# A fused attention and expert kernel on one Trainium2 core: v's two local heads on blocks of 32 partitions, zero halves kept in place, the strided weights reordered by the multiplication with 1/sum

## The chip, the cores and the metric

The kernel runs on one core of one Trainium2 chip. The metric is the device time in microseconds (us), the median of several runs. Beside the runs, one execution was taken by the hardware profiler; its times, and the views worked out from it, are what this document calls the profile. Engines: PE multiplies matrices (PEld is its weight load), DVE, ACT and POOL work element by element, SP issues the DMAs (SPq is its queue).

## What is computed

Attention with 8 batches of 8 heads (576 positions, 64 wide), the first four heads with a window of 32 positions ("local"), the other four with every 32nd position ("strided"). Then a layer of 8 experts (w1, w2) with a capacity of 80 rows each; a row goes to its best expert or stays zero.

```python
def _attn_ref(q, k, v):                      # B, H, S, D = 8, 8, 576, 64
    scores = scale * np.matmul(q, k.transpose(0, 1, 3, 2))
    mask_local = (rel >= 0) & (rel < 32)
    mask_strided = (rel >= 0) & (pos[None, :] % 32 == pos[:, None] % 32)
    masks = np.stack([mask_local if h < H // 2 else mask_strided for h in range(H)], axis=0)
    scores = np.where(masks[None, :, :, :], scores, -1000000000.0)
    scores = scores - np.max(scores, axis=-1, keepdims=True)
    attn = np.exp(scores)
    attn = attn / (np.sum(attn, axis=-1, keepdims=True) + 1e-09)
    return np.matmul(attn, v).astype(np.float32)

def _moe_ref(x, w_gate, w1, w2, capacity):   # x: 4608 x 512, 8 experts, 1024 wide, capacity 80
    logits = x @ w_gate
    expert_idx = np.argmax(logits, axis=1)
    ...
    for e in range(E):
        ...                                  # the 80 rows of e with the largest gate weight
        h = np.maximum(x[tok_idx] @ w1[e], 0.0)
        out[tok_idx] = gate_w[tok_idx, None] * (h @ w2[e])
```

## The kernel before

**Stages.** For each of the 8 batches: q and k are loaded (L617, L620) into `raw` buffers; for the local heads pairs of heads are interleaved by a copy (L401 on POOL, L403 on DVE); PE transposes them (L646), and the transposes are moved from PSUM by ACT or DVE. k is stored twice, each time with the other head's 64 partitions zero, by a multiplication with the 0/1 columns `km` (`masked`: one ACT instruction for each half, L410, or one DVE instruction for both, L417). Local scores (L726 and L735) and strided scores (L809, L816) go through the same `softmax`: the row maximum is subtracted, ACT takes the exp (L692), DVE the row sum (L693) over the weights and a column that holds 1e-9, then 1/sum (L695), and DVE or POOL multiplies (L703). The weights are transposed (L760 local, L834 strided), moved from PSUM with `masked` once more (by `um` local, by `hm` strided), and multiplied with v (L783, L855). The logits of the experts follow (L870, L876), and the output rows are transposed (L952) and stored to a DRAM tensor `xs` (L975, L997).

**v.** For the local heads v lies in one buffer, `vlb`. Its partitions 64 to 127 hold 32 positions each of two heads, and its partitions 0 to 63 the same one block of 32 positions earlier, so that one product covers the window. Eight DMAs of 80 or 64 KB in packets of 256 bytes load it (L671), and a copy fills the lower half from the upper (one for each of two parts, L401 or L403). The two heads alternate from partition to partition: head `u` is written to partitions `64 + u`, `66 + u` and so on. For the strided heads, v goes to 72 partitions next to each other (L683).

**Experts.** The 64 chunks of w1 and w2 (L578, L580) are split into two float16 halves, high (L590 on ACT, L592 on POOL) and low (L598 and L599 on POOL, L601 on DVE). 20 chunks are split before the choice of the rows (from about 417 us), the others between the matrix products of the experts (L1212 to L1214).

**What sets the order.** `program` lists all operations with their readers, writers, a rank and the time that each engine is thought to need (`t_pool`, `t_dve`, `PAR`); `plan` goes through them, gives each the engine that can begin it first and a buffer, and so fixes the order on every engine in advance. `emit` then writes the instructions in that order. All buffers of `program` are pieces of one tile, `K.arena`; the semaphore waits between instructions are put in afterwards, by the framework, from the regions of the tile that each instruction reads and writes.

Of the kernel before, what the change touches and what calls it, by code (L numbers as in the profile page):

```python
# [9 lines left out]
BF16 = mybir.dt.bfloat16  # L10
# [249 lines left out]
def t_pool(n, x=0.0):  # L260
    return 0.15 + 0.001 * n + x
# [6 lines left out]
def program(K, par):  # L268
# [14 lines left out]
    def pool(name, n, count, fifo=True):  # L283
        return Pool(name, [flat(carve(n), n) for _ in range(count)], fifo)
# [17 lines left out]
    plp = pool("pl", 650, 3)  # L302
    psp = pool("ps", 304, 3)
    r4 = end[0]
# [8 lines left out]
    lts = pool("lt", 288, 4)  # L313
    gas = pool("ga", 360, 2)
# [57 lines left out]
    hm, um, km, sel16 = c("hm"), c("um"), c("km"), c("sel16")  # L372
# [33 lines left out]

    def masked(e, o, i, m, n):
# [43 lines left out]
    def c5(e):  # L451
        e.tensor_reduce(K.hm, K.ident.rearrange("p (s z) -> p z s", z=4), op=ALU.add, axis=AX.X)
        e.tensor_reduce(K.um, K.ident.rearrange("p (s z) -> p z s", z=2), op=ALU.add, axis=AX.X)
# [6 lines left out]
    dve(0.9, c5, [ident], [hm, um, km], -99)  # L460
# [6 lines left out]
    def ceps(e):  # L467
        for p in plp.aps:
            e.memset(p().rearrange("p (c n) -> p c n", n=130)[:, :, 128:130], EPS)
        for p in psp.aps:  # L470
            e.memset(p().rearrange("p (g n) -> p g n", n=76)[:, :, 72:76], EPS)

    pol(0.9, ceps, [], [eps], -58)
    pol(0.2, lambda e: e.memset(K.arena[:, kto:kto + 32], 0.0), [], [c("pad")], -90)
    pol(0.4, lambda e: e.memset(vlb().rearrange("p (t h d) -> p t h d", h=2, d=D)[0:64, 0], 0.0), [],  # L475
        [(vlb, "z")], -57)
# [55 lines left out]
    tk = static(lambda: K.tk)  # L532
# [102 lines left out]
    def transposes(src, g, which, rank):  # L635
# [4 lines left out]
        for j3 in range(3):  # L640
# [7 lines left out]
            pe(0.335, f, [src, ident], [t], rank + 0.01 * j3, 128, claim=[dst])  # L648

            def ev(e, t=t, j3=j3):  # L650
# [11 lines left out]
            else:  # L662
                add([("ACT", 1.05), ("DVE", 0.95)], ev, [t, km], [(dst, j3)], rank + 0.5 + 0.01 * j3)
        return dst

    def loadv(b, rank_l, rank_s):
        v4 = lambda: vlb().rearrange("p (t h d) -> p t h d", h=2, d=D)
        for m, (t0, t1) in enumerate(VT):
            for u in range(2):
                for h in range(2):  # L670
                    dma(2.75 * (t1 - t0) / 72, lambda e, u=u, h=h, t0=t0, t1=t1: e.dma_start(  # L671
                        v4()[64 + u:128:2, t0:t1, h],
# [16 lines left out]
    def softmax(p, mx, parts, n, view, ps, rank, tt):  # L689
# [3 lines left out]
        dve(t_dve(tt * 1.02), lambda e: e.tensor_reduce(sm()[:, 0:n], view("eps"), op=ALU.add, axis=AX.X),  # L693
            [p, eps], [sm], rank + 1)
        dve(0.18, lambda e: e.reciprocal(sm()[:, 0:n], sm()[:, 0:n]), [sm], [sm], rank + 1.2)  # L695

        def mul(e):
# [3 lines left out]
            if len(pv.shape) == 4:  # L701
                s = s.rearrange("p (c u) -> p c u", u=pv.shape[2])
            eng.tensor_tensor(pv, pv, s.unsqueeze(len(s.shape)).broadcast_to(list(pv.shape)), op=ALU.mult)  # L703

        add([("POOL", t_poolb(tt) if tt != 288 else 0.66), ("DVE", t_dve(tt))], mul, [p, sm], [p], rank + 1.5)

    def local_scores(b, it, qt, kt, rank):
# [4 lines left out]
        def view(kind):  # L712
            a = p()[:, 0:130 * (t1 - t0)].rearrange("p (c n) -> p c n", n=130)
            if kind == "all":
                return a[:, :, 0:128]
            a = a.rearrange("p c (k u) -> p c u k", u=2)
            return a[:, :, :, 0:64] if kind == "p" else a

        for j, (c0, c1) in enumerate(CGR[it]):
            s = bank()  # L720

            def f(e, s=s, c0=c0, c1=c1):
                w = 128 * (c1 - c0)
# [18 lines left out]
            sv = lambda s=s, w=w: s()[:, 0:w].rearrange("p (t c) -> p t c", c=64)  # L742
# [3 lines left out]
                view("p")[:, c0 - t0:c1 - t0], s()[:, 0:w].rearrange("p (c u k) -> p c u k", u=2, k=64),  # L746
                mx()[:, o:o + nn].rearrange("p (c u) -> p c u", u=2).unsqueeze(3).broadcast_to([P, c1 - c0, 2, 64]),
# [4 lines left out]
    def local_values(b, it, p, xl, rank):  # L752
        t0, t1 = CGR[it][0][0], CGR[it][-1][1]
        pt = Buf(pls_)
        for j, (c0, c1) in enumerate(CGR[it]):
            t = bank()

            def f(e, t=t, c0=c0, c1=c1):
                for cc in range(c0, c1):
                    e.transpose(t()[:, P * (cc - c0):P * (cc - c0) + P],  # L760
                                p()[:, 130 * (cc - t0):130 * (cc - t0) + 128], K.ident)
# [9 lines left out]
            add([("ACT", 2 * t_act(n) - 0.1), ("DVE", t_dve(2 * n))], ev, [t, um], [(pt, j)], rank + 0.5 + 0.2 * j)  # L771
        for j, (c0, c1) in enumerate(CGR[it]):
# [14 lines left out]
            vr = [(vlb, ("p", m)) for m in ms] + [(vlb, ("o", m, u, h)) for m in ms for u in range(2) for h in range(2)]  # L787
# [697 lines left out]
```

## Time and profile before

| | us |
|---|---|
| median of 3 runs | 537.05 |
| lowest, highest | 536.18, 541.28 |
| the profiled execution | 540.64 |
| its span (first to last instruction) | 538.9 |
| PE, DVE, ACT, POOL busy in it | 294.7, 255.4, 189.1, 210.0 |
| mean clock granted to PE | 0.731 |

The span has five stages: the first loads (to about 40 us), the batches (to 417), the choice of the rows for each expert (to 440), the experts (to about 530) and the last store. A busy time is the union of an engine's instructions; matrix products overlap, and their ends are modelled. Idle time before an instruction is put down to the event that came last, here written "<- engine, tile, line", "DMA arena<-v" for a load of v into the arena. In a table by stage, the columns are: from and to, length, busy time and number of instructions of each engine, granted clock, mean busy share of the 16 DMA engines, GB/s.

### The profile page before, as it was taken

To read this page: it belongs to the slowest core of one execution; us is meant where nothing else is said; L and a number is where in the kernel's file an instruction comes from. 1 tells how busy PE (TensorE), PEld (TensorE's weight loads), DVE (VectorE), ACT (ScalarE), POOL (GpSimd) and SP (SyncE) were. 2 spreads that over 40 slices of the span, in tenths; PEclk is the share of its full clock that TensorE was granted. 3 is DMA by queue.
4 is the path that set the end of the run, shared out by engine and by line. 5 is a ranking of instruction groups with operands and counts; after the bars stand their busy time and mean duration, and the time that the engine had idled before them with its cause. 6 is when DMAs were issued, how large, how long until landed. Compare 5 with 4: busy or idle time off the path is not lost. (4 is left out here: it accounts for less than half of the span.)

```text
span 538.9 us, 12588 instructions
## 1 busy us (share of the span) xinstructions
PE 294.7 (55%) x5344; PEld 264.9 (49%) x5344; DVE 255.4 (47%) x430; ACT 189.1 (35%) x334; POOL 210.0 (39%) x188
## 2 busy tenths in 40 slices
PE   3581295129405790285248318703975537997773
PEld 3570175028404680274247217703854437997773
DVE  1382165127313731274148315622695972996730
ACT  0341144033303331243136215311575403865521
POOL 3410083032023212142140222201077676999991
PEclk8596679558955865588659857855895656999886
DMA  6461086128204830194039207611978594887801
GB/s 200 122 245 24 15 271 202 23 74 275 97 22 133 252 128 22 31 314 140 22 92 330 65 13 237 221 24 29 311 240 278 183 327 142 247 291 275 273 26 41
DMA packets 56432, 84.26 MB, mean 156 GB/s; under 512 B 23346, under 2 KB 32564, under 8 KB 56372
## 3 DMA queue, kind: packets, MB, share of 16 engines
q1 hardware_dynamic: 55348, 80.79, 46.8%
q0 software_dynamic: 1024, 2.62, 1.6%
q8 instruction: 44, 0.72, 0.6%
q14 instruction: 16, 0.13, 0.1%
HBM read 63.21 MB, written 20.19 MB: 155 GB/s over the span
## 5 line engine op out<-in xcount | busy, mean ns | idle before, releaser
L401 POOL TENSOR_SCALAR arena<-arena 128x1152 f32<-128x1152 f32 (+3 forms) x30 | 31.5, 1053 | 110.4 <-DMA arena<-v 75.6
L952 PE MATMUL bank<-ident,arena 128*128 128x128 f32 x144 | 28.4, 345 | 78.7 <-DMA arena<-v 63.4
L599 POOL TENSOR_TENSOR arena<-arena 128x1024 f16<-128x1024 f32 x31 | 70.0, 2257 | 2.6
L1213 PE MATMUL bank<-arena 128*128 128x80 f16 x512 | 63.0, 211 | 4.9 <-DVE arena L1208 2.7
L1212 PE MATMUL bank<-arena 128*128 128x80 f16 x512 | 63.3, 211 | 3.6 <-issue 2.3
L1214 PE MATMUL bank<-arena 128*128 128x80 f16 x512 | 62.9, 211 | 2.8 <-POOL arena L599 2.8
L646 PE MATMUL bank<-ident,arena 128*128 128x128 f32 x288 | 56.0, 361 | 14.2 <-DVE arena L403 11.2
L601 DVE SCALAR_TENSOR_TENSOR arena<-arena 128x1024 f16<-128x1024 f32 x33 | 56.4, 1739 | 14.3 <-POOL arena L592 7.8
L952 PEld LDWEIGHTS bank<-ident,arena 128*128 128x128 f32 x144 | 22.1, 191 | 83.4 <-issue 82.9
L410 ACT ACTIVATE arena<-bank,km 128x384 f32<-128x384 f32 x68 | 38.8, 650 | 65.3 <-DMA arena<-v 39.6
L397 ACT COPY arena<-bank 128x512 f32<-128x512 f32 (+4 forms) x64 | 32.7, 513 | 79.5 <-DMA arena<-v 23.5
L1214 PEld LDWEIGHTS <-arena 128*128 128x128 f16 x512 | 54.1, 106 | 8.6 <-issue 5.2
L646 PEld LDWEIGHTS bank<-ident,arena 128*128 128x128 f32 x288 | 50.0, 195 | 15.7 <-POOL arena L475 11.4
L1212 PEld LDWEIGHTS <-arena 128*128 128x128 f16 x512 | 54.2, 106 | 2.6 <-issue 2.6
L1213 PEld LDWEIGHTS <-arena 128*128 128x128 f16 x512 | 54.2, 106 | 1.4 <-issue 1.3
L598 POOL TENSOR_SCALAR arena<-arena 128x1024 f32<-128x1024 f32 x31 | 38.5, 1241 | 39.6 <-DMA arena<-v 25.8
L834 PE MATMUL bank<-ident,arena 128*72 128x128 f32 x64 | 15.2, 385 | 64.5 <-DVE arena L703 64.4
L590 ACT ACTIVATE arena<-arena 128x1024 f16<-128x1024 f32 x44 | 44.6, 1054 | 16.6 <-DMA arena<-moe_w 12.7
L592 POOL TENSOR_SCALAR arena<-arena 128x1024 f16<-128x1024 f32 x20 | 26.4, 1320 | 52.1 <-DMA arena<-v 28.0
L693 DVE TENSOR_REDUCE arena<-arena 128x16 f32<-128x304 f32 (+2 forms) x32 | 23.1, 729 | 42.9 <-DMA arena<-v 42.8
L703 POOL TENSOR_TENSOR arena<-arena 128x288 f32<-128x288 f32 (+1 forms) x7 | 7.3, 1045 | 90.2 <-DMA arena<-v 55.2
L834 PEld LDWEIGHTS bank<-ident,arena 128*72 128x72 f32 x64 | 8.2, 154 | 67.9 <-ACT arena L399 36.6
(170 smaller groups left out, 597.8 us busy)
## 6 DMA issues: line engine op xcount, KB each, us to landing
arena<-moe_w SPq DMA_DIRECT2D x64, 512.0 KB
arena<-q SPq DMA_DIRECT2D x16, 576.0 KB
arena<-k SPq DMA_DIRECT2D x16, 576.0 KB
out<-arena SPq DMA_DIRECT2D x18, 512.0 KB
xs<-arena SPq DMA_DIRECT2D x16, 512.0 KB
arena<-v SPq DMA_DIRECT2D x16, 288.0 KB
arena<-v SPq DMA_DIRECT2D x32, 80.0 KB
arena<-v SPq DMA_DIRECT2D x32, 64.0 KB
```

Source lines behind the costliest of these rows:

```text
L397: K.nc.scalar.copy(o, i)
L401: K.nc.gpsimd.tensor_scalar(o, i, 1.0, 0.0, op0=ALU.mult, op1=ALU.add)
L410: K.nc.scalar.activation(o(z), i, AF.Copy, scale=m[:, z:z + 1])
L590: K.nc.scalar.activation(part(0), st(), AF.Copy, scale=SC)
L598: K.nc.gpsimd.tensor_scalar(st(), st(), SC, 0.0, op0=ALU.mult, op1=ALU.add)
L599: K.nc.gpsimd.tensor_tensor(part(1), st(), part(0), op=ALU.subtract)
L601: K.nc.vector.scalar_tensor_tensor(part(1), st(), SC, part(0), op0=ALU.mult, op1=ALU.subtract)
L646: e.transpose(t()[:, P * jj:P * jj + P], cp[:, 3 * j3 + jj], K.ident)
L952: e.transpose(t()[:, P * k:P * k + P], src[half][1](k), K.ident)
L1212: e.matmul(o, w[:, 0, i:i + P], x[:, 0], start=first, stop=False)
L1213: e.matmul(o, w[:, 0, i:i + P], x[:, 1], start=False, stop=False)
L1214: e.matmul(o, w[:, 1, i:i + P], x[:, 0], start=False, stop=last)
```

## The change

- **Local v.** Head `u` now lies on partitions `64 * u + 32` to `64 * u + 63`, and its earlier block on the 32 partitions below. The copy of the earlier block becomes two, one for each head. The columns of the local weights are ordered head by head (`(u k)`, not `(k u)`), so that their transposes fit; `um` goes, `km` serves.
- **Zero halves.** The halves of `ktl`, `kst` and `ptl` that are always zero are set once at the start. ACT then copies only the 64 partitions that differ (`halves_of`); DVE multiplies both halves as before.
- **1e-9.** The local weights lose their two extra columns a chunk (640 for 650 elements); 16 additions, one for each local softmax, add 1e-9 to the sums on DVE or POOL. Strided weights keep a column.
- **Strided weights.** They stay in the order of the scores until the multiplication with 1/sum, which writes them to a second buffer (`pq`) in the order that the transposes need.
- **Memory.** `oh` moves into the arena on top of `lt`, and `tk` onto `gates`.
- **Planner.** Its times for POOL and for two DVE multiplications change.

```diff
 def t_pool(n, x=0.0):
-    return 0.15 + 0.001 * n + x
+    return 0.1 + 0.00093 * n + x
...
-    plp = pool("pl", 650, 3)
+    plp = pool("pl", 640, 3)
     psp = pool("ps", 304, 3)
+    pqp = pool("pq", 288, 2)
...
+    def halves_of(e, o, i):
+        if e == "ACT":
+            for x in range(2):
+                K.nc.scalar.copy(o(x)[64 * x:64 * x + 64], i[64 * x:64 * x + 64])
+        else:
+            masked(e, o, i, K.km, 2)
...
+    for i, (o, n, rk) in enumerate(((kto + 32, 2 * S, -89), (kss.off, 2 * S, -56), (pls_.off, 640, -55),
+                                    (pls_.off + 1280, 640, -20))):
+        for x in range(2):
+            add([("POOL", t_pool(n)), ("DVE", 0.1 + 0.00055 * n)],
+                lambda e, o=o, n=n, x=x: (K.nc.gpsimd if e == "POOL" else K.nc.vector).memset(
+                    K.arena[64 * x:64 * x + 64, o + n * (1 - x):o + n * (2 - x)], 0.0), [], [(pads[i if i < 3 else 3], x)], rk)
...
-                    masked(e, lambda z: d if z is None else d[:, z], tv, K.km, 2)
+                    halves_of(e, lambda z: d if z is None else d[:, z], tv)
...
                     dma(2.75 * (t1 - t0) / 72, lambda e, u=u, h=h, t0=t0, t1=t1: e.dma_start(
-                        v4()[64 + u:128:2, t0:t1, h],
+                        v4()[64 * u + 32:64 * u + 64, t0:t1, h],
...
-            add([("POOL", t_pool(nn)), ("DVE", 0.1 + 0.00065 * nn)],
-                lambda e, a0=a0, t1=t1: copy(e, v4()[0:64, a0:t1], v4()[64:128, a0 - 1:t1 - 1]),
-                own, [(vlb, ("p", m))], rank_l + 3 + m * par["vm"])
+            for u in range(2):
+                add([("POOL", t_pool(nn)), ("DVE", 0.1 + 0.00065 * nn)],
+                    lambda e, a0=a0, t1=t1, u=u: copy(e, v4()[64 * u:64 * u + 32, a0:t1],
+                                                      v4()[64 * u + 32:64 * u + 64, a0 - 1:t1 - 1]),
+                    [x for x in own if x[1][2] == u], [(vlb, ("p", m, u))], rank_l + 3 + m * par["vm"])
...
-        dve(t_dve(tt * 1.02), lambda e: e.tensor_reduce(sm()[:, 0:n], view("eps"), op=ALU.add, axis=AX.X),
-            [p, eps], [sm], rank + 1)
+        if tt == 288:
+            dve(t_dve(tt * 1.02), lambda e: e.tensor_reduce(sm()[:, 0:n], view("eps"), op=ALU.add, axis=AX.X),
+                [p, eps], [sm], rank + 1)
+        else:
+            dve(t_dve(tt), lambda e: e.tensor_reduce(sm()[:, 0:n], view("sum"), op=ALU.add, axis=AX.X),
+                [p], [sm], rank + 1)
+            add([("DVE", 0.19), ("POOL", 0.22)], lambda e: (K.nc.gpsimd if e == "POOL" else K.nc.vector).tensor_scalar(
+                sm()[:, 0:n], sm()[:, 0:n], EPS, 0.0, op0=ALU.add, op1=ALU.add), [sm], [sm], rank + 1.1)
...
+            if ps is None:
+                eng.tensor_tensor(pv, pv, s.broadcast_to(list(pv.shape)), op=ALU.mult)
+            else:
+                o = ps().rearrange("p (g c z) -> p g z c", g=4, z=4)
+                i = pv.rearrange("p (g z) c -> p g z c", z=4)
+                s = s.rearrange("p (g z) o -> p g z o", z=4)
+                eng.tensor_tensor(o, i, s.broadcast_to([P, 4, 4, 18]), op=ALU.mult)
...
-            if kind == "all":
-                return a[:, :, 0:128]
-            a = a.rearrange("p c (k u) -> p c u k", u=2)
-            return a[:, :, :, 0:64] if kind == "p" else a
+            if kind == "all":
+                return a
+            return a.rearrange("p (t k) -> p t k", k=64)
...
-                masked(e, lambda z: d if z is None else d[:, z], tv, K.um, 2)
+                halves_of(e, lambda z: d if z is None else d[:, z], tv)
...
-    hiA=[("ACT", 1.06), ("POOL", 1.15)], loA=[("DVE", 1.39), ("POOL", 2.85)],
+    hiA=[("ACT", 1.06), ("POOL", 1.05)], loA=[("DVE", 1.39), ("POOL", 3.15)],
...
-    cp=[("POOL", 1.3), ("DVE", 0.85)],
+    cp=[("POOL", 1.25), ("DVE", 0.85)],
```

How this moves the instructions is seen in the order on each engine. In the rows below, "waits" names the semaphores that an instruction waits for: PE, DVE, Activation (ACT) and Pool for those engines, DMAHW0 to DMAHW7 for the eight lanes that SP's DMAs use in turn (the end _49 is part of the names). A number of lines is 29 or so higher in the changed kernel.

SP, the first loads, before (L617 and L620 load q and k, L671 v):

```order
L620 DMA arena<-q 128x1152
L620 DMA arena<-k 128x1152
L485 DMA wgt<-moe_w_gate 128x2x8 [waits DVE_49]
L671 DMA arena<-v 32x10x64 [waits DMAHW2_49,DMAHW3_49,DMAHW1_49,DMAHW0_49]
L671 DMA arena<-v 32x10x64 x3
L671 DMA arena<-v 32x8x64 x3
L671 DMA arena<-v 32x8x64 [waits DMAHW4_49,DVE_49,Pool_49]
```

The same place in the changed kernel (L634 and L637 load q and k, L689 v, L502 the gate's weights):

```order
L637 DMA arena<-q 128x1152
L637 DMA arena<-k 128x1152
L689 DMA arena<-v 32x10x64 x4
L689 DMA arena<-v 32x8x64 [waits DMAHW0_49]
L689 DMA arena<-v 32x8x64 [waits DMAHW1_49]
L689 DMA arena<-v 32x8x64 [waits DMAHW2_49]
L689 DMA arena<-v 32x8x64 [waits DMAHW3_49]
L502 DMA wgt<-moe_w_gate 128x2x8 [waits DMAHW4_49,DVE_49]
```

The first load of v stood behind the lanes of all four loads of q and k; now the first four loads of v have no wait, and the others wait for one lane each.

SP, the loads of v for the second batch, before, and the load of k behind them:

```order
L671 DMA arena<-v 32x10x64 [waits DMAHW1_49,DMAHW3_49,DMAHW0_49,DMAHW4_49,DVE_49,DMAHW5_49,PE_49,DMAHW7_49,Activation_49,Pool_49]
L671 DMA arena<-v 32x10x64 [waits DVE_49,Activation_49]
L671 DMA arena<-v 32x10x64 [waits Activation_49]
L671 DMA arena<-v 32x10x64 [waits DVE_49,DMAHW6_49,Activation_49,Pool_49]
L671 DMA arena<-v 32x8x64 [waits DVE_49,Activation_49]
L671 DMA arena<-v 32x8x64 [waits Pool_49]
L671 DMA arena<-v 32x8x64 [waits PE_49]
L671 DMA arena<-v 32x8x64 [waits DMAHW2_49,DVE_49,Activation_49]
L617 DMA arena<-k 128x2x576 [waits DMAHW4_49,DMAHW5_49,DMAHW3_49,DMAHW6_49,DMAHW2_49,DMAHW7_49,DMAHW1_49,DMAHW0_49]
```

and in the changed kernel (L569 writes zeros to the output):

```order
L689 DMA arena<-v 32x10x64 [waits DMAHW2_49,DVE_49,PE_49]
L689 DMA arena<-v 32x10x64 [waits DMAHW3_49,PE_49]
L689 DMA arena<-v 32x10x64 [waits DMAHW4_49]
L689 DMA arena<-v 32x10x64 [waits DMAHW5_49]
L689 DMA arena<-v 32x8x64 [waits DMAHW6_49,PE_49]
L689 DMA arena<-v 32x8x64 [waits DMAHW7_49,PE_49]
L689 DMA arena<-v 32x8x64 [waits DMAHW0_49]
L689 DMA arena<-v 32x8x64 [waits DMAHW1_49]
L569 DMA out<-arena 512x1x256 [waits DMAHW2_49]
L634 DMA arena<-k 128x2x576 [waits DMAHW3_49,Pool_49]
```

Each load waited for up to four engines; now four of the eight wait for PE, one of these for DVE too, and all for one lane.

DVE, the end of the first batch, from the strided scores on, before (L822 subtracts the maximum, L693 to L703 are the softmax, L417 masks):

```order
L822 TENSOR_TENSOR arena<-bank_82,arena 128x4x4x18 [waits DVE_49]
L822 TENSOR_TENSOR arena<-bank_75,arena 128x4x4x18 [waits DVE_49]
L403 COPY arena<-bank_80 128x2x128 [waits PE_49,Activation_49]
L693 TENSOR_REDUCE arena<-arena 128x16 [waits DMAHW7_49,DMAHW0_49,Activation_49]
L693 TENSOR_REDUCE arena<-arena 128x16 [waits DMAHW1_49,Activation_49,Pool_49]
L695 RECIPROCAL arena<-arena 128x16 [waits DVE_49] x2
L703 TENSOR_TENSOR arena<-arena 128x4x4x18 [waits DMAHW2_49,DVE_49]
L403 COPY arena<-arena 128x4x32 [waits DMAHW3_49,Activation_49]
L405 TENSOR_SCALAR arena<-bank_76 128x128x3 [waits DMAHW4_49,PE_49]
L417 TENSOR_TENSOR arena<-bank_77,hm 72x1152 [waits DMAHW5_49,PE_49]
L417 TENSOR_TENSOR arena<-bank_80,km 128x256x3 [waits DMAHW6_49,PE_49,Activation_49]
```

and in the changed kernel (L852, L714 to L734, L429):

```order
L852 TENSOR_TENSOR arena<-bank_79,arena 128x16x18 [waits DVE_49]
L408 COPY arena<-bank_78 128x2x128 [waits PE_49]
L851 TENSOR_REDUCE arena<-bank_77 128x16
L714 TENSOR_REDUCE arena<-arena 128x16 [waits Activation_49]
L852 TENSOR_TENSOR arena<-bank_77,arena 128x16x18 [waits DVE_49]
L721 RECIPROCAL arena<-arena 128x16 [waits DVE_49]
L734 TENSOR_TENSOR arena<-arena 128x4x4x18 [waits DVE_49]
L714 TENSOR_REDUCE arena<-arena 128x16 [waits Activation_49]
L721 RECIPROCAL arena<-arena 128x16 [waits DVE_49]
L734 TENSOR_TENSOR arena<-arena 128x4x4x18 [waits DVE_49]
L429 TENSOR_TENSOR arena<-bank_79,km 128x256x3 [waits PE_49]
L429 TENSOR_TENSOR arena<-bank_81,km 128x256x3 [waits PE_49]
```

The sums, multiplications and maskings named the lanes of DMAs one after the other (DMAHW7, 0, 1, 2 up to 6); now they name only the engines whose results they use. The copies of v's earlier block are 16 before, 10 of them on POOL and 6 on DVE, and 32 after, 15 on POOL and 17 on DVE. Of the 16 additions of 1e-9, 7 stand on POOL and 9 on DVE. Between the choice of the rows and the end POOL had 14 low and 7 high halves of the weights and has 13 and 6, DVE had 30 low halves and has 31.

More of the change, by code (lines that the diff above doesn't have):

```diff
@@ L283, in pool @@
     def pool(name, n, count, fifo=True):
-        return Pool(name, [flat(carve(n), n) for _ in range(count)], fifo)
+        off = end[0]
+        p = Pool(name, [flat(carve(n), n) for _ in range(count)], fifo)
+        p.off = off
+        return p
     def static(ap):
@@ L459, in program @@
     dve(0.15, lambda e: e.tensor_copy(K.identb, K.ident), [ident], [identb], -100)
-    dve(0.9, c5, [ident], [hm, um, km], -99)
+    dve(0.9, c5, [ident], [hm, km], -99)
     warm(par["warm0"], -200)
@@ L648, in transposes @@
             pe(0.335, f, [src, ident], [t], rank + 0.01 * j3, 128, claim=[dst])
+            zeros = [] if which == 0 else [pads[0], pads[0]] if g == 0 else [pads[1]]
             def ev(e, t=t, j3=j3):
@@ L662, in transposes @@
             else:
-                add([("ACT", 1.05), ("DVE", 0.95)], ev, [t, km], [(dst, j3)], rank + 0.5 + 0.01 * j3)
+                add([("ACT", 1.02), ("DVE", 0.96)], ev, [t, km, *zeros], [(dst, j3)], rank + 0.5 + 0.01 * j3)
         return dst
@@ L700, in mul @@
             s = sm()[:, 0:n]
[L701 to L705, printed above, removed]
+            s = s.unsqueeze(2)
+            if ps is None:
[5 more added lines that the diff above has]
+                eng.tensor_tensor(o, i, s.broadcast_to([P, 4, 4, 18]), op=ALU.mult)
+        if ps is None:
+            add([("POOL", t_poolb(tt)), ("DVE", 0.2 + 0.00105 * tt)], mul, [p, sm], [p], rank + 1.5)
+        else:
+            add([("POOL", 0.83), ("DVE", 0.68)], mul, [p, sm], [ps], rank + 1.5)
     def local_scores(b, it, qt, kt, rank):
@@ L760, in f @@
                     e.transpose(t()[:, P * (cc - c0):P * (cc - c0) + P],
[L761 removed]
+                                p()[:, P * (cc - t0):P * (cc - t0) + P], K.ident)
             pe(0.112 * (c1 - c0), f, [p, ident], [t], rank + 0.2 * j, 128, claim=[pt])
@@ L768, in ev @@
                 tv = t()[:, 0:P * (c1 - c0)].rearrange("p (c n) -> p c n", n=P)
-                masked(e, lambda z: d if z is None else d[:, z], tv, K.um, 2)
-            add([("ACT", 2 * t_act(n) - 0.1), ("DVE", t_dve(2 * n))], ev, [t, um], [(pt, j)], rank + 0.5 + 0.2 * j)
+                halves_of(e, lambda z: d if z is None else d[:, z], tv)
+            add([("ACT", 2 * t_act(n) - 0.1), ("DVE", t_dve(2 * n))], ev, [t, km, pads[2], pads[3]], [(pt, j)], rank + 0.5 + 0.2 * j)
         for j, (c0, c1) in enumerate(CGR[it]):
@@ L833, in f @@
             for g in range(4):
-                e.transpose(t()[0:72, P * g:P * g + P], p()[:, 76 * g:76 * g + 72], K.ident)
+                e.transpose(t()[0:72, P * g:P * g + P], p()[:, 72 * g:72 * g + 72], K.ident)
         pe(0.45, f, [p, ident], [t], rank, 128, claim=[pt])
@@ L1133, in program @@
         [(small, 0), (slot, "s"), jc], [(slot, "b")], z + 0.5)
-    oh, tab = c("oh"), bank()
+    oh, tab = Buf(Pool("oh", [None], True, [(lts,)])), bank()
     for j0 in (0, 8):
@@ L1305 @@
     vm=2.0, mstep=4.0, mx=2.0, mf=5.0, gland=6.3,
-    hiA=[("ACT", 1.06), ("POOL", 1.15)], loA=[("DVE", 1.39), ("POOL", 2.85)],
-    hiB=[("ACT", 1.06), ("POOL", 1.15)], loB=[("DVE", 1.39), ("POOL", 2.85)],
-    cp=[("POOL", 1.3), ("DVE", 0.85)],
+    hiA=[("ACT", 1.06), ("POOL", 1.05)], loA=[("DVE", 1.39), ("POOL", 3.15)],
+    hiB=[("ACT", 1.06), ("POOL", 1.05)], loB=[("DVE", 1.39), ("POOL", 3.15)],
+    cp=[("POOL", 1.25), ("DVE", 0.85)],
     rank=dict(lq=-16.0, cp=-6.0, tl=0.0, ls=-8.0, vl=-6.0, vs=0.0, sl=3.0, sx=1.0, ts=6.0, pl=8.0, pli=1.5, ss=10.0,
@@ L1341, in moe_attention @@
     mk(work, "identb", [P, P], BF16)
-    mk(work, "mloc", [P, 10, 64], BF16)
+    mk(work, "mloc", [P, 5, P], BF16)
     mk(work, "mstr", [P, 16, 18], BF16)
@@ L1345, in moe_attention @@
     K.wgl, K.wgs = K.wgt[:, 0], K.wgt[:, 1]
-    for name, n in (("hm", 4), ("um", 2), ("km", 2), ("sel16", 16), ("segm", NSEG), ("esel", E), ("jc", NCAND),
+    for name, n in (("hm", 4), ("km", 2), ("sel16", 16), ("segm", NSEG), ("esel", E), ("jc", NCAND),
                     ("jc1", NCAND), ("capf", 2), ("lim", 1), ("tb", 3), ("tbd", 2), ("cv", NCAND), ("gv2", 288),
@@ L1364, in moe_attention @@
     K.val = work.tile([P, NCAND, E, 5], BF16, name="val")
-    tkt = mk(work, "oht", [P, NCAND * SLOTS // 2])
-    K.oh = tkt.bitcast(BF16).rearrange("p (j s) -> p j s", s=SLOTS)
-    K.tk = tkt[0:1, 0:48 * E].rearrange("p (n e) -> p n e", e=E)
+    K.oh = K.arena[:, K.oho:K.oho + NCAND * SLOTS // 2].bitcast(BF16).rearrange("p (j s) -> p j s", s=SLOTS)
     mk(work, "pieces", [P, NCAND, 5], BF16)
```

65 lines of the change are left out of this document (32 added, 33 removed).

## The prediction

> **What bounds the kernel now.** I read the page first, then the waits of the engines and of SP's own queue, then the timeline of one place and the busy times by stage. The page's busy tenths in 40 slices (13.5 us each):
>
> ```profile
> span 538.9 us, 12588 instructions
> PE   3581295129405790285248318703975537997773
> PEclk8596679558955865588659857855895656999886
> DMA  6461086128204830194039207611978594887801
> ```
>
> PE is not full before the last quarter. PE and DMA rise and fall together in some seven waves, so something stops them at once. The waits name it (waiting instruction <- releaser: us in total, times, longest):
>
> ```profile
> POOL arena L401 <- DMA arena<-v: 75.6, 10, 21.2
> DVE arena L693 <- DMA arena<-v: 42.8, 10, 8.1
> ACT arena L692 <- DMA arena<-v: 40.8, 7, 9.9
> ```
>
> L692 and L693 are the exp and the row sum of the softmax: they neither read nor write v, and yet they wait for a load of v. SP's queue shows the other direction, the v loads of L671 waiting for such work:
>
> ```profile
> SPq L671 <- DVE arena L693: 21.2, 8, 2.8
> ...
> SPq L671 <- ACT arena L410: 14.6, 5, 3.8
> ...
> SPq L671 <- PE bank L783: 5.0, 3, 4.2
> ```
>
> In time (start, duration, engine; in brackets the idle time before and its releaser), batch 1's eight loads:
>
> ```profile
> 39.84 27.00 SPq L671 DMA_DIRECT2D arena<-v  x8
> 42.31 0.59 ACT L397 COPY arena<-bank 128x512 f32<-128x512 f32 x1 [2.93 <-DMA arena<-v]
> ...
> 45.77 0.56 ACT L399 ACTIVATE arena<-bank 128x384 f32<-128x384 f32 x1 [2.87 <-DMA arena<-v]
> 48.87 0.56 ACT L399 ACTIVATE arena<-bank 128x384 f32<-128x384 f32 x1 [2.54 <-DMA arena<-v]
> ```
>
> Load, an instruction or two per engine, next load: a lockstep with a beat of about 3.1 us. The orders shown above agree: each v load waits for several engines, and the arena instructions behind it wait for one load's lane after the other. The loads with this trouble are those that write every second partition (64 + u to 128); I infer that the dependency tracking counts such a destination as meeting everything in the arena. The v loads of L683, on adjacent partitions, have only PE to wait for. Busy time by stage: the seven lockstep windows (first, last, sum of all seven), and the seven stretches between and after them:
>
> ```profile
> core 0: us, PE busy (x) PEld busy (x) DVE busy (x) ACT busy (x) POOL busy (x), PEclk, DMA share, GB/s
> 39.80:68.60 28.80, 5.26 (x26) 4.19 (x24) 4.11 (x7) 4.05 (x8) 2.29 (x2) 0.63 0.09 20
> 349.80:375.60 25.80, 4.37 (x43) 3.77 (x44) 6.12 (x9) 3.56 (x8) 1.41 (x3) 0.53 0.10 23
> sum 188.60, PE 25.85 PEld 20.69 DVE 29.82 ACT 24.11 POOL 20.80; mean PE 3.69 PEld 2.96 DVE 4.26 ACT 3.44 POOL 2.97
> ```
>
> ```profile
> 68.60:91.40 22.80, 20.25 (x421) 17.28 (x421) 16.98 (x36) 10.78 (x21) 15.70 (x12) 0.86 0.85 273
> 375.60:417.00 41.40, 31.94 (x535) 26.32 (x535) 29.76 (x48) 26.61 (x47) 22.23 (x14) 0.79 0.83 270
> sum 188.60, PE 162.52 PEld 142.97 DVE 130.00 ACT 101.32 POOL 81.78; mean PE 23.22 PEld 20.42 DVE 18.57 ACT 14.47 POOL 11.68
> ```
>
> By chance both sum to 188.60 us. The windows take 35% of the span, with at most 29.82 us of work of one engine in them; in the stretches PE is busy 86% and DVE 69%. So the loads of v bound the attention part, not an engine.
>
> **The change, part by part.** Against the span of 538.9 us.
>
> 1. *Windows, -188.6.* v's heads go to partitions 32 to 63 and 96 to 127, adjacent ones. In the changed order the v loads wait for PE and DVE where they reuse v's buffer, and otherwise for DMA lanes; on DVE only copies and the weights' halves still name a lane, no softmax and no masking. The windows fall whole. What was done in them remains: **+18**. It lies between 0 (all of it fits into holes) and 29.8 (DVE's sum, end to end). I take 18 by two rows: the DMA share of 0.09 to 0.11 over 188.6 us is some 18.7 us of transfers, and PE's 25.85 us at clocks of 0.53 to 0.63 would be some 18 us at the stretches' 0.8 to 0.9. Late next would be DVE.
>
> 2. *Start, -10.* The rows at the start:
>
> ```profile
> 9.31 9.01 SPq L671 DMA_DIRECT2D arena<-v  x8
> 16.30 1.35 DVE L403 COPY arena<-arena 128x1152 f32<-128x1152 f32 x1 [11.94 <-DMA arena<-v]
> ...
> 21.39 5.62 PEld L646 LDWEIGHTS bank<-ident,arena 128*128 128x128 f32 x27 [1.84 <-POOL arena L401]
> ```
>
> The first v load goes out at 9.31, having waited for q and k; so these had landed, but DVE's first copy of q starts at 16.30. Without the tie it starts at 9.3 at the latest, about 5 at the earliest (estimate: a quarter of the first four loads): 7 to 11 us, and the second gap of 1.84 us of PE's weight loads: 7 to 13, taken 10. The memsets that keep zero halves (seven on DVE, one more large one on POOL) lie in this idle time (11.94 us of DVE before 16.30) and cost nothing; without that cover seven at up to 0.86 us (the 64x1152 copy below) would be 6 us, once.
>
> 3. *PE's clock, -11.* PE comes out of each window slow:
>
> ```profile
> 68.60:74.80 6.20, 6.17 (x53) 5.51 (x57) 4.38 (x6) 3.22 (x8) 5.89 (x5) 0.50 0.82 255
> 375.60:382.00 6.40, 6.40 (x52) 5.83 (x53) 2.96 (x4) 3.37 (x7) 1.12 (x1) 0.50 0.83 254
> sum 48.50, PE 47.43 PEld 44.15 DVE 30.34 ACT 27.78 POOL 31.57; mean PE 6.78 PEld 6.31 DVE 4.33 ACT 3.97 POOL 4.51
> ...
> 76.00:80.00 4.00, 4.00 (x152) 3.47 (x148) 3.97 (x8) 1.05 (x2) 3.84 (x3) 1.00 1.01 352
> ```
>
> Seven beginnings of 48.5 us (first and last shown) at or near a clock of 0.50, PE busy throughout, then 1.00. At 1.00 they could take 24 us less (47.43 / 2); but DMA is 82 or 83% busy there too and may set the pace, so 0 to -24, taken near the middle. The Trainium skill, page "TensorE: Matmul & The Clock Gate", part 1, says that the gate passes half the pulses until PE has been busy for about 3.4 us, and again after an idle window of that length. The trace agrees on the halves, not on the length, which is 6.9 us here (48.5 / 7); by the page's 3.4 us the bound would be 12 us (7 x 3.4 / 2), half of it 6, and the sum 5 us higher.
>
> 4. *Added work, +8.* The copy of v's overlap becomes two of half the partitions, and half the partitions cost the same:
>
> ```profile
> L401 POOL TENSOR_SCALAR arena<-arena 128x1152 f32<-128x1152 f32 x15 | 17.8, 1188 | 52.6 <-PE bank L646 28.7 <-DMA arena<-v 18.5 <-issue 2.5
> L401 POOL TENSOR_SCALAR arena<-arena 64x1152 f32<-64x1152 f32 x5 | 5.7, 1149 | 3.8 <-DMA arena<-v 3.5
> ...
> L403 DVE COPY arena<-arena 64x1152 f32<-64x1152 f32 x3 | 2.6, 855 | 0.1
> ...
> L695 DVE RECIPROCAL arena<-arena 128x10 f32<-128x10 f32 x8 | 1.6, 205 | 0.0
> ```
>
> 32 copies for 16: POOL gets 15 (it had 10), +5.5 us at 1.1, hidden by its idle half; DVE 17 (it had 6), 11 more at 0.86: +10 us. The 1e-9 is 16 additions of about 0.2 us (as the reciprocal), nine on DVE: +1.8. Other strided weightings and maskings change between DVE, POOL and ACT; as their counts go both ways I take nothing for them but 2 us more in the upper end. So 0 to 14. DVE would be busy 130 + 30 + 12 of about 204 us, 84%, not always on the path: taken 8. ACT's masking by a scale becomes a copy of 64 partitions each: taken at nothing, as ACT is busy 101 of 188.6 us in the stretches. Reading sums over adjacent columns and dropping the two 1e-9 columns: nothing (640 elements for 650, an estimate of 1.5% of such a sum).
>
> 5. *The experts, -3.* From 440 on, POOL is the fullest (first to last columns as above), and its pairs for the weights' low halves (L598, L599) vary:
>
> ```profile
> 440.00:538.90 98.90, 70.71 (x1602) 68.32 (x1601) 55.52 (x58) 45.47 (x69) 78.40 (x48) 0.85 0.59 195
> ...
> L598 POOL TENSOR_SCALAR arena<-arena 128x1024 f32<-128x1024 f32 x31 | 38.5, 1241 | 39.6 <-DMA arena<-v 25.8 <-ACT arena L590 11.9
> ...
> L599 POOL TENSOR_TENSOR arena<-arena x31: 1995/2122/2992, 69.8 to 522.6; 128x1024 f16<-128x1024 f32 x31
> ```
>
> The new costs of the planner leave POOL 13 low halves there for 14 and six high halves for seven, DVE 31 low halves for 30. One pair less is 3.2 to 4.2 us (1.24, and L599's 2.0 to 3.0), a high half less one more: 0 to -5, taken -3. Choosing the experts (417 to 440) is unchanged.
>
> **Sum:** 538.9 - 188.6 + 18 - 10 - 11 + 8 - 3 = 352.3 us of span. The profiled execution took 540.64 us, 1.7 above its span and 0.7% above the median of 537.05: 354 against it, **352** against the median.
>
> **Rivals.** *A: DVE becomes the bound.* With everything packed, DVE and POOL meet more often, and one shape of instruction on DVE has these durations (ns, min/median/max):
>
> ```profile
> L601 DVE SCALAR_TENSOR_TENSOR arena<-arena x33: 1204/1527/3162, 399.7 to 520.4; 128x1024 f16<-128x1024 f32 x33
> ```
>
> Then the windows' 29.8 us of DVE come end to end, the 14 us in full, and the clock brings nothing since PE waits: 538.9 - 188.6 + 29.8 - 10 + 14 - 3 = 381. For it: DVE is busy 3.97 of 4.00 us in 76 to 80. Against: PE, not DVE, is full at the stretches' beginnings. The Trainium skill, "SBUF — State Buffer", "Who interferes with whom", says that a DVE instruction with two SBUF inputs and a GpSimd one that reads SBUF exclude each other for a whole instruction; the spread from 1.2 to 3.2 us agrees, and by that rule A is what denser packing brings.
>
> *B: the clock stays up and the holes take the work.* -24 for the clock, +5 for the windows' work, +2 added, -13 start, -5 experts: 315. For it: PE is full at 0.50 in every beginning. Against: the DMA share of 1.01 in 76 to 80, which no clock relieves.
>
> *C: the windows stay.* If small packets and not the false waits made the beat, the loads would still take 27 us for eight, about 537. Against: they have a DMA share of 0.1, one in flight.
>
> *D: slower.* v has one buffer; its first load waits for PE's products of the batch before, and q and k of the next batch queue behind it on SP. Should that wait reach the 27 us of a window, nothing is won and the 16 extra copies at 1.1 us lie on it: 555. Against: in SP's waits L671 waits 5.0 us in all for those products (L783), three times.
>
> **Numbers.** Forecast 0.58 (its own range 336 to 368), A 0.24, B 0.14, C 0.02, D 0.02. The time is the forecast's, 352. The range 322 to 387 takes in all of the forecast and most of A and B. One per cent is about what a measurement of this kernel can tell from no change: faster by more 0.96, within 0.02 (C), slower 0.02 (D).
>
> **What would show it.** Term 1: no softmax instruction waits for v, eight v loads issued within some 5 us, periods of 24 to 29 us for 51.6 (28.80 + 22.80). Term 2: DVE's first copy before 10 us. Term 3: the mean clock above 0.8 (0.73 now). Term 4: 32 copies at 0.85 to 1.15 us. Term 5: from the choice of experts to the end 117 to 122 us. Wrong: a new common wait in every batch, a DVE busy over 95% of the attention part (A), or one where PE never waits (B).

## The result, and the profile after

The changed kernel takes 351.38 us (median of four runs, 347.91 to 356.38) beside 538.45 us for the kernel before on the same chip: ratio 0.650, 95% interval 0.644 to 0.657. A second job gave 0.651 (0.647 to 0.656). The forecast was 352. The profiled execution took 356.38 us, the longest of its four; its sums are read with that in mind.

The page of the changed kernel, the span and the busy tenths in 40 slices (8.9 us each now):

```profile
span 354.7 us, 12582 instructions
PE   4679959959969696987989976946529994969690
DVE  7897887969948978988979887489924994795900
PEclk9696998969977988999998997556658998998897
DMA  7974996966984885898887898568775979895011
```

The seven valleys of PE and DMA are gone; in the attention part (slices 1 to 26) PE, DVE and DMA stand side by side, mostly at 6 to 9, and none is at 9 throughout. The changed kernel's timeline, the v loads of the first batches and of the last on SP's queue (start, us from the first issue to the end of the last, number):

```profile
3.11 7.00 SPq L689 DMA_DIRECT2D arena<-v  x8
30.59 3.83 SPq L689 DMA_DIRECT2D arena<-v  x8
57.27 4.19 SPq L689 DMA_DIRECT2D arena<-v  x8
...
191.95 3.84 SPq L689 DMA_DIRECT2D arena<-v  x8
```

From batch 1 on, eight loads go out in 3.8 to 5 us where they took 23 to 27, and a batch comes every 26.9 us ((191.95 - 30.59) / 6). The waits of its engines (waiting <- releaser: us in total, times, longest), three of the longest of the engines outside the experts, then the two longest of SP's queue:

```profile
POOL arena L719 <- DVE arena L717: 35.6, 5, 9.3
...
ACT arena L402 <- PE bank L982: 23.6, 9, 4.9
...
POOL arena L406 <- DVE arena L721: 16.6, 3, 5.8
```

```profile
SPq L1005 <- ACT arena L402: 37.2, 10, 9.0
SPq L689 <- PE bank L816: 30.1, 8, 5.6
```

No softmax instruction waits for a load of v any more. New at the head is a tiny one: POOL stands before the addition of 1e-9 (L719) until DVE has its row sum (L717). On SP, v's single buffer now waits for PE's products of the batch before (L816) for 30.1 us in all, 4.3 us for each of the seven batches that reuse it, where it was 5.0 in all.

By stage, columns as in the prediction's windows. First the kernel before, then the changed one: up to batch 1's v loads, from there to the first MAX8 (where the choice of the experts' rows begins), and the rest.

```profile
0.00:39.80 39.80, 23.10 (x396) 21.53 (x397) 18.16 (x36) 11.79 (x21) 13.24 (x43) 0.79 0.59 192
39.80:418.40 378.60, 188.79 (x3241) 163.85 (x3238) 161.19 (x291) 126.78 (x238) 102.58 (x80) 0.70 0.44 139
418.40:538.90 120.50, 82.85 (x1710) 79.53 (x1710) 76.03 (x103) 50.55 (x75) 94.15 (x65) 0.80 0.61 200
```

```profile
0.00:30.60 30.60, 20.43 (x358) 19.09 (x360) 25.06 (x43) 10.95 (x19) 15.89 (x43) 0.82 0.80 232
30.60:237.00 206.40, 173.02 (x3288) 152.09 (x3285) 167.66 (x310) 126.11 (x256) 118.53 (x94) 0.87 0.81 258
237.00:354.70 117.70, 81.15 (x1706) 78.44 (x1704) 76.52 (x105) 51.66 (x75) 91.13 (x62) 0.83 0.62 203
```

The middle falls from 378.6 to 206.4 us with nearly the same work in it: the DMA share rises from 0.44 to 0.81, the granted clock from 0.70 to 0.87. PE's own busy time falls by 15.8 us, for 47 more matmuls. The start gives 9.2 us, the end 2.8.

### The profile page after: what moved, and what is told of

It reads as the page before. It is cut to its first block, busy times and chain, and to the rows that moved or that the text cites. A ratio compares the mean times of both kernels' runs of the same rounds, so it can differ in the third digit from the quotient of the medians.

```text
span 354.7 us, 12582 instructions
## 1 busy us (share of the span) xinstructions
PE 274.6 (77%) x5344; PEld 249.6 (70%) x5344; DVE 269.2 (76%) x455; ACT 188.7 (53%) x349; POOL 225.5 (64%) x199
## 5 line engine op out<-in xcount | busy, mean ns | idle before, releaser
L406 POOL TENSOR_SCALAR arena<-arena 128x1152 f32<-128x1152 f32 (+3 forms) x38 | 40.5, 1071 | 35.4 <-DVE arena L721 16.6
L415 ACT COPY arena<-bank 64x384 f32<-64x384 f32 (+2 forms) x86 | 45.4, 528 | 16.5 <-PE bank L793 13.5
L663 PE MATMUL bank<-ident,arena 128*128 128x128 f32 x288 | 42.2, 299 | 5.2 <-DVE arena L408 5.2
L663 PEld LDWEIGHTS bank<-ident,arena 128*128 128x128 f32 x288 | 37.1, 157 | 5.9 <-POOL gates L550 5.4
L846 PE MATMUL bank<-arena 128*18 128x36 f32 x1024 | 23.0, 250 | 16.2 <-issue 15.9
L846 PEld LDWEIGHTS bank<-arena 128*18 128x18 f32 x1024 | 20.5, 120 | 18.1 <-issue 17.0
L408 DVE COPY arena<-bank 128x288 f32<-128x288 f32 (+4 forms) x38 | 19.8, 523 | 13.9 <-PE bank L816 7.3
L429 DVE TENSOR_TENSOR arena<-bank,km 128x768 f32<-128x768 f32 (+2 forms) x29 | 27.0, 950 | 3.2 <-PE bank L793 1.8
L712 ACT ACTIVATE arena<-arena 128x288 f32<-128x288 f32 (+2 forms) x32 | 18.2, 572 | 16.7 <-DVE arena L778 10.5
L816 PE MATMUL bank<-arena 128*64 128x64 f32 x576 | 24.3, 252 | 3.3 <-issue 3.3
```

Of the source, the lines that this page charges most:

```text
L406: K.nc.gpsimd.tensor_scalar(o, i, 1.0, 0.0, op0=ALU.mult, op1=ALU.add)
L415: K.nc.scalar.copy(o(x)[64 * x:64 * x + 64], i[64 * x:64 * x + 64])
L663: e.transpose(t()[:, P * jj:P * jj + P], cp[:, 3 * j3 + jj], K.ident)
L846: e.matmul(so[32 * h:32 * h + 18, rr, :, z], q_[:, h, r::16], k_[:, :, h, r::16], start=False, stop=(rr == 1 and z == 3), tile_position=(0 ...
```

## The experiments

Ratios are against the kernel before, run beside each; one hundredth is some 5.4 us.

**e1: v on blocks alone.** The kernel before, with the destination of the loads and the two copies changed. Local weights are in blocks too (otherwise the products would not fit v); the 1e-9 isn't added to the local sums. No zero halves kept, no strided reorder, old costs.

```diff
-                        v4()[64 + u:128:2, t0:t1, h],
+                        v4()[64 * u + 32:64 * u + 64, t0:t1, h],
...
-            return a[:, :, :, 0:64] if kind == "p" else a
+            if kind == "p":
+                return a[:, :, 0:128].rearrange("p c (u k) -> p c u k", u=2)
+            return a[:, :, 0:128].rearrange("p c (u k) -> p c u k", u=2)
```

> The kernel before with v's two heads on blocks of 32 partitions (local weights ordered head by head, two copies of the earlier block) and nothing else of the change; the zero halves are masked as before, the planner's costs are the old ones; the 1e-9 is not added to the local sums. Theory (the every-second-partition destination makes the false waits): the lockstep windows go, 345 to 365 us. Rival (the zero halves, the reordered strided weights or the new planner costs carry a good part): 380 us or more. Rival (small packets): about 537.

Measured: 352.44 us, ratio 0.655 (0.651 to 0.659). That is the whole gain within the intervals: the rest of the change together makes no difference that these runs can tell (0.655 against 0.650). That rest holds the 16 additions of 1e-9, which e1 leaves out (see e4).

**e2: the transfer left as it was, the tile alone.** The kernel before; v keeps every second partition, but lies in a tile of its own. For the room, two halves of the experts' weights are split ahead, not three (`npre`, not shown).

```diff
-    vlb = static(flat(carve(4 * S), 4 * S))
+    carve(4 * S)
+    vlb = static(lambda: K.vlt)
...
+    mk(work, "vlt", [P, 4 * S])
```

> The kernel before with v's buffer as a tile of its own, the destination still every second partition; for the room, two halves of expert weights are split ahead instead of three. Theory (the tracking counts this destination as meeting everything in its tile): the windows go though the transfers are the same, 345 to 375 us. Rival (256-byte packets to 64 partitions are slow by themselves): the eight loads still take about 27 us a batch, 520 to 550 us.

Measured: 357.68 us, ratio 0.665 (0.661 to 0.669). Its timeline, SP's queue:

```profile
25.19 5.58 SPq L672 DMA_DIRECT2D vlt<-v  x8
...
52.07 5.83 SPq L672 DMA_DIRECT2D vlt<-v  x8
```

The same transfers to the same partitions take 5.6 us for eight, not 25. So neither the packets nor the partitions are slow: it takes both, a destination of every second partition and a tile that everything else lives in, for the loads and the arena's work to wait for each other. From batch 1's v loads to the first MAX8 e2 and e1 take 204.3 us each (25.19 to 229.50, 24.71 to 229.00); what e2 is slower by lies behind the MAX8 (126.3 us for 120.4).

**e3: the change without the blocks.** The changed kernel, v on every second partition again, local weights interleaved, one copy of 64 partitions.

```diff
-                        v4()[64 * u + 32:64 * u + 64, t0:t1, h],
+                        v4()[64 + u:128:2, t0:t1, h],
...
-                halves_of(e, lambda z: d if z is None else d[:, z], tv)
+                masked(e, lambda z: d if z is None else d[:, z], tv, K.um, 2)
```

> The changed kernel with v alone put back (every second partition, one copy of the earlier block, local weights with the heads alternating, masked by um). Theory: the windows come back, 525 to 550 us. Rival (the other parts carry the gain): below 450 us.

Measured: 498.43 us (one run). The windows are back; its timeline on SP's queue, and its waits:

```profile
78.98 22.24 SPq L689 DMA_DIRECT2D arena<-v  x8
...
123.65 24.39 SPq L689 DMA_DIRECT2D arena<-v  x8
...
222.43 14.17 SPq L689 DMA_DIRECT2D arena<-v  x6
```

```profile
POOL arena L406 <- DMA arena<-v: 92.1, 10, 22.3
...
DVE arena L712 <- DMA arena<-v: 57.7, 12, 9.7
```

The direction holds, the size doesn't: I expected 525 at least. The loads of batches 1 to 7 take 149.9 us on SP here, for 174.3 before (two batches send two loads outside the lockstep). The spans, 496.6 for 538.9, differ by 42 us: 24 are these loads, 5 the start (batch 1's first load of v at 34.83 for 39.84), 2 the part behind the MAX8 (118.2 us for 120.5). The other 11 are unexplained. My guess, not tested, is that a false wait costs what the order puts behind it.

**e4: without the additions.** The changed kernel without the 16 additions of 1e-9. Each local sum holds exp(0) = 1, so 1e-9 lies below float32's resolution.

```diff
-            add([("DVE", 0.19), ("POOL", 0.22)], lambda e: (K.nc.gpsimd if e == "POOL" else K.nc.vector).tensor_scalar(
-                sm()[:, 0:n], sm()[:, 0:n], EPS, 0.0, op0=ALU.add, op1=ALU.add), [sm], [sm], rank + 1.1)
```

> The changed kernel without the 16 additions of 1e-9 to the local sums (each sum is 1 or more, as the largest weight is exp(0)). If the added work on the softmax chain is on the path (DVE 83 per cent busy, POOL waiting 35.6 us for sums in its five longest waits): 343 to 349 us. Rival (off the path): 350 to 353 us.

Measured: 340.94 us, ratio 0.632 (0.628 to 0.636). Sixteen instructions that the page of the changed kernel prices at about 7 us in all were worth 10, with the order that goes with them (15 copies of v's blocks stand on DVE here, 17 in the changed kernel). e1 leaves out the 1e-9 too: beside it (0.655) the rest of the change gains 0.023, some 12 us. So e1 comes out beside the changed kernel since this gain and the cost of the additions about cancel.

**e5: the changed kernel again**, beside e6 to e8.

> The changed kernel itself, unaltered, as the measure for the three kernels beside it: 348 to 354 us, DVE's first copy of the start at about 10 us, the first MAX8 of the choice of rows at 230 to 237 us.

Measured: 355.47 us, ratio 0.651 (0.647 to 0.656); the median is above the 348 to 354 expected, as the kernel before also ran higher in this job (541.72). First copy at 10.06, MAX8 at 235.72.

**e8: all additions on DVE.** The changed kernel, `("POOL", 0.22)` struck from the addition's choices.

> The 16 additions of 1e-9 all on DVE, none in POOL's in-order queue (seven stood there). Theory (an addition costs by standing behind POOL's work of 1 to 3 us; the chain of row sum, addition and reciprocal stays on one engine otherwise): 342 to 347 us. Rival (the addition's cost is the slot and the chain wherever it stands): 350 to 353 us, as the unaltered changed kernel.

Measured: 345.92 us, ratio 0.637 (0.633 to 0.640). Most of what e4 gained is had by taking seven additions off POOL. But the planner also moved other work: DVE copies 12 of the 32 blocks of v here and 17 in the changed kernel. Whether POOL's queue behind the addition costs the 8 us, or the order that goes with it, these runs don't separate.

**e7: no additions, no zero halves.** As e4; the memsets of halves are gone, and ACT writes both halves of a masked tile with a scale of 0 or 1.

```diff
-            for x in range(2):
-                K.nc.scalar.copy(o(x)[64 * x:64 * x + 64], i[64 * x:64 * x + 64])
+            masked(e, o, i, K.km, 2)
```

> Without the 16 additions, and with the zero halves taken out: no memsets of halves, and ACT writes both halves of a masked tile whole with a scale of 0 or 1, as before. Theory (a half of the partitions costs ACT as much as all of them: 64x1152 in 1149 ns beside 128x1152 in 1188 ns, so the zero halves save nothing and cost the start 5 us): 335 to 341 us, DVE's first copy near 5 us. Rival (the zero halves are what made the changed kernel without additions 11.5 us faster than v on blocks alone, 340.9 beside 352.4): 348 to 354 us.

Measured: 334.78 us, ratio 0.618 (0.615 to 0.621): 7 us less than e4, and the fastest kernel of this study. As in e4, only the 1e-9 below float32's resolution is left out. Here the zero halves cost time (e11 tries it again). The two durations in the expectation are POOL's copies, not ACT's. ACT's own, in the changed kernel, say much the same: a copy of 64x512 takes 577 ns, one of 128x512 589. Its halves are a little cheaper all the same (64x384 by a copy 540 ns in the changed kernel, 128x384 by a scale 668 ns here), but batch 1's v loads come at 24.12 us here and at 29.64 in e4.

**e6: no additions, three memsets later.** As e4, with the memsets of the strided k tile and of the two local weight tiles ranked at 0 and 3 (from -56, -55 and -20).

> Without the 16 additions of 1e-9 (each local sum holds exp(0) = 1, so 1e-9 lies below float32's resolution), and with the memsets of the strided k tile and of the two local weight tiles ranked later, so that DVE's first copies stand ahead of three of them. Theory (the seven memsets ahead of DVE's first copies lie on the path of the start, at some 5 us): the first copy of DVE comes before 8 us, batch 1's v loads 2 to 4 us earlier, 335 to 339 us beside the 340.9 without the additions alone. Rival (the start is hidden in the schedule behind it, since 'memsets cost nothing'): 340 to 343 us.

Measured: 346.26 us, ratio 0.635 (0.631 to 0.639), no gain over e4. The start did as the theory said (first copy at 7.21, batch 1's v loads at 26.06), but the MAX8 came at 226.24, later than e4's 218.62. The 3.6 us won at the start did not arrive at the end; neither the theory's range nor the rival's holds the 346.26.

**e9 and e12: the planner's costs of before** for POOL (those of two DVE multiplications stay new), once in e7 and once in the changed kernel.

```diff
-    return 0.1 + 0.00093 * n + x
+    return 0.15 + 0.001 * n + x
...
-    hiA=[("ACT", 1.06), ("POOL", 1.05)], loA=[("DVE", 1.39), ("POOL", 3.15)],
+    hiA=[("ACT", 1.06), ("POOL", 1.15)], loA=[("DVE", 1.39), ("POOL", 2.85)],
...
-    cp=[("POOL", 1.25), ("DVE", 0.85)],
+    cp=[("POOL", 1.3), ("DVE", 0.85)],
```

> As the kernel without additions and without zero halves (334.8 us, ratio 0.618), with the planner's costs of before (a POOL copy of n elements 0.15 + 0.001 n in place of 0.1 + 0.00093 n, POOL's high half 1.15 and low half 2.85 in place of 1.05 and 3.15, a copy of v 1.3 in place of 1.25). Theory (the new costs only shift a few instructions between POOL and DVE): 332 to 339 us, ratio 0.613 to 0.626. Rival (the costs carry a good part of the 18 us by which this kernel beats v on blocks alone, since a planned low half on POOL at 2.85 draws work to POOL): 342 to 350 us.

> The changed kernel with the planner's costs of before and nothing else altered (the same edit that cost 12 us, ratio 0.618 to 0.641, in the kernel without additions and zero halves). Theory (with the windows gone, no single engine is the bound, and another order of the same work moves the time by some us either way, so the edit is worth something else here): ratio 0.640 to 0.662, 345 to 356 us. Rival (the new costs are worth 12 us wherever they stand, since they describe POOL better): ratio 0.668 to 0.680, 360 to 367 us.

Measured: e9 344.97 us, ratio 0.641 (0.638 to 0.645), 12 us slower than e7: the rival there. e12 354.09 us, ratio 0.654 (0.649 to 0.659), the same as the changed kernel: the theory there. One edit, which changes no instruction's work, is worth 12 us in one surrounding and nothing in the other.

**e10: the strided softmax as before**, in e7: interleaved weights, 1/sum multiplied in place.

```diff
-            view("p"), sv(), mx().unsqueeze(2).broadcast_to([P, 16, 18]), op=ALU.subtract),
+            view("p"), s()[:, 0:288].rearrange("p (g z c) -> p g z c", z=4, c=18),
+            mx().rearrange("p (g z) -> p g z", z=4).unsqueeze(3).broadcast_to([P, 4, 4, 18]), op=ALU.subtract),
```

> As the kernel without additions and without zero halves (334.8 us), with the strided softmax as before: the subtraction writes the weights interleaved (18x4 with a step of 4), the row sum reads them interleaved, and 1/sum multiplies in place; no tile of its own for the reordered weights. Theory (the strided reorder is a good part of the 18 us): 342 to 350 us, ratio 0.632 to 0.647. Rival (it is worth nothing that can be measured; the order of the local columns and the planner's costs carry them): 333 to 337 us.

Measured: 344.43 us, ratio 0.636 (0.632 to 0.640), 10 us slower than e7. The groups by line and shape show what the reorder saves. The row sum (L707) and the subtraction in e10 (L850), then in e7 (L707, L843):

```profile
L707 DVE TENSOR_REDUCE arena<-arena 128x16 f32<-128x304 f32 x16 | 10.9, 698 | 1.7 <-ACT arena L705 1.6
L850 DVE TENSOR_TENSOR arena<-bank,arena 128x288 f32<-128x288 f32 x16 | 10.7, 699 | 0.0
```

```profile
L843 DVE TENSOR_TENSOR arena<-bank,arena 128x288 f32<-128x288 f32 x16 | 7.1, 448 | 0.1
...
L707 DVE TENSOR_REDUCE arena<-arena 128x16 f32<-128x304 f32 x16 | 7.0, 455 | 1.1 <-ACT arena L705 1.0
```

Written with a step the subtraction takes 699 ns, in a row 448; read with a step the row sum takes 698 ns, in a row 455. That is 7.5 us of DVE. Against it e7 has 13 of the multiplications on DVE and e10 ten (12.8 us and 9.3). How much of the 10 us is this and how much the order isn't told apart.

**e11: zero halves out, additions kept on DVE.**

> The whole computation of the changed kernel with the 16 additions of 1e-9, but these all on DVE and the zero halves taken out (ACT writes both halves with a scale of 0 or 1, no memsets of halves). If the two savings add (0.6512 to 0.6367 by the additions' engine, 0.6319 to 0.6184 by the zero halves): ratio 0.623, 337 us, range 334 to 341. Rival (an addition in DVE's row at the start takes back what the memsets leave): 343 to 347 us.

Measured: 342.83 us, ratio 0.636 (0.633 to 0.639). Just below the rival's range: it is no faster than e8 (0.637), so what the zero halves cost between e4 and e7 they don't cost here, though the v loads of batch 1 come early again (24.18 us; 28.97 in e8).

## Why the prediction came out, by its steps

The mechanism, the windows, was right and is shown. That the sum meets the measured time within 1 us is in part luck: the start came right by errors that cancel, and the parts of the added work didn't hold.

**Windows (-188.6, +18), clock (-11), added work (+8).** From batch 1's v loads to the MAX8 these make -173.6, and -172.2 was measured. e1, e2 and e3 show the cause: blocks alone give all of it, a tile of its own gives nearly all, and the old destination takes most of it back. That the dependency tracking is what ties the loads, which the prediction inferred, fits all three; no run looks at the tracking itself. The split of the sum into its parts isn't shown: the clock term is supported by PE's busy time of the middle, 15.8 us less for 47 more matmuls, and by the mean clock of 0.854 (over the 0.8 asked for), but no run held the clock apart.

**Start (-10; 9.2 measured).** Right by two errors that cancel. The gain without memsets was put too low, and the memsets were put at nothing. q was there as early as the lower of the two bounds, about 5: e1 copies it at 4.95 and e7 at 4.93, and their batch 1 loads come at 24.71 and 24.12, 15 us earlier than before, where 7 to 13 were forecast. The changed kernel gives some 6 of these back, by the step "the memsets lie in this idle time and cost nothing". DVE at the start of the changed kernel, in its timeline:

```profile
2.49 1.02 DVE L489 MEMSET arena<- 64x1152 f32 x1 [0.18 <-issue]
3.78 1.02 DVE L489 MEMSET arena<- 64x1152 f32 x1 [0.28 <-issue]
4.99 1.02 DVE L489 MEMSET arena<- 64x1152 f32 x1 [0.19 <-issue]
...
9.42 0.59 DVE L489 MEMSET arena<- 64x640 f32 x1 [0.17 <-issue]
10.04 1.35 DVE L408 COPY arena<-arena 128x1152 f32<-128x1152 f32 x1
```

From 1.52 on DVE is idle for 0.3 us at most at a time ahead of the copy at 10.04, so this check fails by a little (asked: before 10). The cover that I named, 11.94 us of idle DVE, was the wait for v, which the same change removes. The fallback price in the prediction, "6 us, once", was the right one for the start. What it is worth at the end is less sure: 7 us by e4 and e7, nothing by e8 and e11.

**Added work (+8).** No run measures the size by itself, and the parts don't hold. The additions were put at 1.8 us of DVE; the nine there take 5.3 us, and all 16 cost 10 us of the kernel (e4), 8 of which go when the seven leave POOL and the order changes with them (e8). On the copies the prediction's check fails: it asked for 0.85 to 1.15 us each. The changed kernel's groups by line and shape:

```profile
L408 DVE COPY arena<-arena 32x1152 f32<-32x1152 f32 x9 | 12.0, 1332 | 0.3
...
L406 POOL TENSOR_SCALAR arena<-arena 32x1024 f32<-32x1024 f32 x8 | 9.5, 1185 | 1.0 <-DMA arena<-v 0.5
L406 POOL TENSOR_SCALAR arena<-arena 32x1152 f32<-32x1152 f32 x7 | 8.8, 1257 | 1.8 <-DMA arena<-v 1.4
L408 DVE COPY arena<-arena 32x1024 f32<-32x1024 f32 x8 | 7.4, 922 | 0.2
```

The 17 on DVE take 19.4 us where the six before took 5.7: +13.7, not +10. Counts were as said, durations grew with the packing: with POOL idle, at 198.66, two copies on DVE take 1.36 us together; at 118.91, beside a POOL instruction that runs from 118.35 to 120.87, one takes 2.58. On the other side stand the strided weights: the sums read in a row, which the prediction took at nothing, and the subtractions, which it left out, take 14.2 us of DVE in the changed kernel (446 and 448 ns each) for 21.4 before (690 and 695). In e7's surroundings this part and POOL's new costs gained 10 and 12 us; in the changed kernel the costs gained nothing (e12), and the strided part wasn't tried there.

**Experts (-3).** 117.7 us from the MAX8 to the end, for 120.5: -2.8. With the costs of before it is 120.4 in e1, 121.3 in e9 and 123.0 in e12; with the new ones 117.5 to 119.6 in e3, e5 to e8, e10 and e11. So the costs are the likely cause, though e4 has 121.8 with the new ones.

**The rivals.** A: DVE is not full. The changed kernel's busy times by stage, the sum over its first 192 us (to the end of batch 6):

```profile
sum 192.00, PE 157.86 PEld 141.63 DVE 158.73 ACT 107.78 POOL 105.65; mean PE 19.73 PEld 17.70 DVE 19.84 ACT 13.47 POOL 13.21
```

DVE is busy 83%, for the 84% worked out, and PE as much. What A fears, DVE held up by POOL, is there in the copies above, but not enough to make DVE the bound. B: PE is busy for 173.0 of the middle's 206.4 us, so it still waits, and the clock there is 0.87, not 1. C is refuted by e2. D's wait came, 4.3 us a batch, and stayed far below the 27 from which it would decide: only copies wait for v.

## What to carry to other kernels

Look among the waits for instructions that wait for a load they don't use; here a destination of every second partition in a tile that everything shares cost 187 us, and either adjacent partitions or a tile of its own removes it. When a step is priced at nothing because it lies in idle time, ask whether the same change removes that idle time. Where no engine is full and a planner sets the order, edits worth some 10 us need not add up (7 us and 8 us here, e7 and e8, came to 8 together, e11): time each in the kernel in which it will stay.

## What was not expected of the hardware

A tiny addition on DVE can wait out a whole instruction of POOL. In e8, DVE's timeline (start, duration), then POOL's over the same stretch:

```profile
121.00 1.02 DVE L719 TENSOR_SCALAR arena<-arena 128x10 f32<-128x10 f32 x1
...
124.46 1.40 DVE L719 TENSOR_SCALAR arena<-arena 128x8 f32<-128x8 f32 x1
```

```profile
120.94 1.05 POOL L609 TENSOR_SCALAR arena<-arena 128x1024 f16<-128x1024 f32 x1 [3.70 <-DMA arena<-moe_w]
...
123.24 2.59 POOL L616 TENSOR_TENSOR arena<-arena 128x1024 f16<-128x1024 f32 x1
```

The additions end at 122.02 and 125.86; POOL's instructions, which began first, end at 121.99 and 125.83. One more of the 16 does the same (99.77 to 100.78, POOL's to 100.76). Where POOL is idle (144.82) the same addition takes 0.17 us. The reciprocal behind it, of the same shape, never waits: 189 to 254 ns over all 32 in the changed kernel, 0.19 us at 25.37 in the midst of a POOL instruction (24.67 to 26.46). The Trainium skill, "SBUF — State Buffer", "Who interferes with whom", says that a `tensor_scalar` on DVE can enter a mode that shares its ports with GpSimd, and that whichever issues first blocks the other for its whole instruction; these rows agree to within 0.03 us. So an addition of a constant is not priced by its size beside a busy POOL, and the reciprocal, from which the prediction read its 0.2 us, was the wrong neighbour: the nine on DVE in the changed kernel take 0.17 to 1.38 us.
